# A polynomial over a polynomial after linear attention: one projected term, additions moved to accumulating DMAs, paired attention tiles, and a fixed issue order

## The chip, the cores and the metric

The kernel runs on one core of a Trainium2 chip. The metric is the device time of one execution in microseconds (us), lower being better. The core has a matrix engine (TensorE, PE in the profile for matmuls and PEld for weight loads), a vector engine (VectorE, DVE), a scalar engine (ScalarE, ACT), GpSimd (POOL), which issues the accumulating DMAs here, SyncE (SP), which issues the loads and stores, and 16 DMA engines that all queues share. Each engine works through its own list of instructions in order. Tiles lie in SBUF, the on-chip memory; TensorE's results land in PSUM, from where another engine copies them out (an "evacuation"). "Granted clock" is the share of TensorE's full clock that the profile shows as granted. Executions are called fast or slow: a run more than 1.5% above the fastest of the same kernel is slow.

## The reference, cut to what matters

```python
# attention: batch 4, heads 4, seq 1088, head_dim 32; S1, S2 are 8 x 32
phi(x) = outer(S1 @ x, S2 @ x)              # 64 features for each row
kv, z  = sum_s phi(k) v,  sum_s phi(k)
attn   = (phi(q) @ kv) / (phi(q) @ z + 1e-6)
# then, for x = attn as 4352 tokens x 128
h = x @ w_in                                # 128 -> 2048
P = a[0] + a[1]*h + a[2]*h**2 + a[3]*h**3
Q = 1 + |b[0]|*|h| + |b[1]|*h**2
out = (P / (Q + 1e-6)) @ w_out              # 2048 -> 128
```

All arrays come and go as float32. Between the two matmuls the kernels work in bfloat16.

## The kernel before

Tokens are taken in eight chunks of 512 and a last one of 256 (the last 64 rows of each batch). A "group" is eight blocks of 128 hidden columns of one chunk, as a tile of 128 x 4096. A few groups, the first and last ones, are smaller; all together are worth 17 full groups. For each group TensorE computes `h` (the "hidden products"), ScalarE copies it to bf16 (`hb`), VectorE makes the polynomials, and ScalarE makes the reciprocal as exp(-ln Q).

```python
# VectorE, for one group (names: m = |h|, u = Q - 1, y = numerator, r = 1/Q)
m = hb & 0x7FFF                                   # abs, by clearing the sign bit
u = m * b1 + b0                                   # tensor_scalar, two scalars
u = u * m                                         # tensor_tensor
y = hb * a3 + a2                                  # tensor_scalar
y = y * hb                                        # tensor_tensor
y = y + a1                                        # tensor_scalar
y = y * hb                                        # tensor_tensor
y = y * r                                         # tensor_tensor, after ScalarE's Ln and Exp
# TensorE: two terms are projected, a0 sits in the first weight
out_ps += (a0 * w_out).T @ r
out_ps += w_out.T @ y
...
# every copy from PSUM is ScalarE's; attention works on one-bank tiles (128 x 512), a pair of heads at a time
class Plan:                                       # a list scheduler at build time
    def issue(self):
        ...
        key = (t, s["rank"], s["n"])              # earliest start, then rank, then number
        ...
# hidden products of group g have rank g - 1.45, its last product g + 0.55
BUFS = dict(xT=3, hb=3, m=1, u=2, r=2, y=2, L=2, h_ps=2, out_ps=1, w_ps=2, kv_ps=1, ...)
```

## Time and profile before

| | before |
|---|---|
| time, median of the runs beside the changed kernel | 329.27 us (323.33 to 333.12, 4 runs; by the 1.5% rule three of them are slow) |
| span of the profiled execution | 323.9 us |
| VectorE busy | 286.5 us, 88% |
| TensorE busy (matmul records) | 280.0 us, 86% |
| ScalarE busy | 228.4 us, 71% |
| DMA engines, share of the steady part | 0.04 |

The page of the kernel before: the busy time of each engine, two rows of the 40 equal slices (a digit is the busy share in tenths), and the chain of waits followed back from the last instruction.

```profile
PE 280.0 (86%) x1153; PEld 150.0 (46%) x1172; DVE 286.5 (88%) x300; ACT 228.4 (71%) x213; POOL 8.7 (3%) x29
...
DVE  1461599999999999999999999999999999999990
...
DMA  5798000200020000000000000000000000000000
...
DVE 77%; PE 13%; DMA 5%; issue 1%; SPq 1%; ACT 1%; DVEq 0%
```

The reader is to see that VectorE is full from slice 6 to slice 39, that the DMA engines have next to nothing to do in that time, and that VectorE is 77% of the chain.

The groups by line of the kernel before, shapes kept apart: busy time, mean ns of one, then the idle time before them.

```profile
L503 DVE TENSOR_TENSOR y<-y,hb 128x4096 bf16<-128x4096 bf16 x30 | 68.7, 2292 | 0.9
L486 DVE TENSOR_TENSOR u<-u,m 128x4096 bf16<-128x4096 bf16 x15 | 34.4, 2292 | 0.4
L510 DVE TENSOR_TENSOR y<-y,r 128x4096 bf16<-128x4096 bf16 x15 | 34.3, 2284 | 0.0
L482 DVE TENSOR_SCALAR u<-m,b_abs 128x4096 bf16<-128x4096 bf16 x15 | 20.2, 1345 | 0.4
L499 DVE TENSOR_SCALAR y<-hb,a_sb 128x4096 bf16<-128x4096 bf16 x15 | 20.1, 1341 | 0.0
L506 DVE TENSOR_SCALAR y<-y,a_sb 128x4096 bf16<-128x4096 bf16 x15 | 19.3, 1286 | 0.5
L476 DVE TENSOR_SCALAR m<-hb 128x4096 int16<-128x4096 int16 x15 | 18.3, 1220 | 0.0
```

A pass with two tensors costs 2.29 us, one with scalars 1.22 to 1.35 us. Eight such passes are 14.35 us for a full group, with next to no idle time before them. This is what the change attacks.

The windows of the kernel before: each row gives its length and then each engine's busy time, the granted TensorE clock, the DMA share and GB/s, for the prologue, the steady part (from VectorE's first pass of group 0 to its last) and the end.

```profile
0.00:35.80 35.80, 30.81 (x144) 18.84 (x147) 11.39 (x34) 9.55 (x16) 6.62 (x27) 0.95 0.74 217
35.80:316.50 280.70, 247.54 (x1004) 130.46 (x1020) 275.12 (x267) 218.07 (x195) 2.09 (x2) 0.97 0.04 12
316.50:323.90 7.40, 1.70 (x6) 0.69 (x5) 0.00 (x0) 0.74 (x2) 0.00 (x0) 0.50 0.08 18
```

In the steady part VectorE (the third busy time of a row) works for 275.1 of 280.7 us.

### The profile page before, as it was taken

The numbers are of one execution on the slowest core, as the hardware profiler recorded it, in microseconds if no ns is written. First come the engines' busy times: TensorE is split into PE (matmuls) and PEld (weight loads), VectorE is DVE, ScalarE is ACT, GpSimd is POOL, SyncE is SP. The second block draws the span as 40 slices with busy tenths as digits, with TensorE's granted clock in tenths as the row PEclk, the third lists the DMA queues.
The fourth block names the chain that finished last, engine by engine and source line by source line (L and its number), as shares of the span: only waits on it lengthen the run. The fifth ranks groups of instructions, "written<-read, shape, count | busy, mean of one in ns | idle before, by whom it ended". The sixth has DMA issues, their size and how long they took to land.

```text
span 323.9 us, 3027 instructions
## 1 busy us (share of the span) xinstructions
PE 280.0 (86%) x1153; PEld 150.0 (46%) x1172; DVE 286.5 (88%) x300; ACT 228.4 (71%) x213; POOL 8.7 (3%) x29
## 2 busy tenths in 40 slices
PE   7969999988899999898999998979999975992532
PEld 4835455555443544555445554645345422650220
DVE  1461599999999999999999999999999999999990
ACT  3122678979479879794798888675989795686650
POOL 4102000002000000000000000000000000000000
PEclk9997999999999999999999999989999999698695
DMA  5798000200020000000000000000000000000000
GB/s 157 222 314 266 0 1 2 65 1 0 25 74 0 0 34 0 0 0 2 32 0 1 34 0 0 0 2 32 0 0 35 0 0 0 0 34 0 0 32 16
DMA packets 12125, 11.20 MB, mean 35 GB/s; under 512 B 4048, under 2 KB 10448, under 8 KB 11984
## 3 DMA queue, kind: packets, MB, share of 16 engines
q1 hardware_dynamic: 12112, 11.02, 11.2%
q8 instruction: 9, 0.15, 0.2%
q14 instruction: 4, 0.03, 0.0%
HBM read 8.79 MB, written 2.23 MB: 34 GB/s over the span
## 4 chain that ended last, share of the span: by engine, by line
DVE 77%; PE 13%; DMA 5%; issue 1%; SPq 1%; ACT 1%; DVEq 0%
DVE y L503 22%; DVE u L486 11%; DVE y L510 10%; DVE y L499 6%; DVE u L482 6%; DVE y L506 6%; PE h_ps L466 6%; DVE m L476 5%; DMA L<-in_moe_w_out_dram 3%; DVE q_pT L398 3%; DVE k_p L314 2%; PE out_ps L517 2%; PE w_ps L405 2%; DMA v_sb<-in_v_dram 2%; PE w_ps L389 2%; DVE x_sb L417 2%
## 5 line engine op out<-in xcount | busy, mean ns | idle before, releaser
L466 PE MATMUL h_ps<-xT,w_in_sb 128*128 128x512 f32 (+1 forms) x288 | 127.7, 584 | 2.7 <-ACT xT L428 2.4
L472 ACT CAST hb<-h_ps 128x1024 bf16<-128x1024 f32 x68 | 67.7, 1013 | 23.6 <-PE h_ps L466 22.8
L490 ACT ACTIVATE L<-u,one_ap 128x2048 f32<-128x2048 bf16 (+1 forms) x35 | 68.4, 1954 | 18.1 <-DVE u L486 18.1
L503 DVE TENSOR_TENSOR y<-y,hb 128x4096 bf16<-128x4096 bf16 (+2 forms) x40 | 78.9, 1972 | 1.2
L466 PEld LDWEIGHTS h_ps<-xT,w_in_sb 128*128 128x128 f32 x288 | 53.3, 194 | 56.3 <-issue 42.3
L495 ACT ACTIVATE r<-L 128x2048 bf16<-128x2048 f32 (+1 forms) x35 | 65.4, 1870 | 0.4
L517 PE MATMUL out_ps<-r,w_out_108 128*128 128x512 bf16 (+1 forms) x139 | 35.6, 378 | 11.6 <-ACT r L495 11.2
L517 PE MATMUL out_ps<-y,w_out_109 128*128 128x512 bf16 (+1 forms) x132 | 34.4, 389 | 10.7 <-DVE y L510 9.9
L486 DVE TENSOR_TENSOR u<-u,m 128x4096 bf16<-128x4096 bf16 (+2 forms) x20 | 39.4, 1971 | 0.6
L510 DVE TENSOR_TENSOR y<-y,r 128x4096 bf16<-128x4096 bf16 (+2 forms) x20 | 39.3, 1965 | 0.1
L517 PEld LDWEIGHTS <-w_out_109 128*128 128x128 bf16 x144 | 14.4, 104 | 32.1 <-issue 21.7
L517 PEld LDWEIGHTS <-w_out_108 128*128 128x128 bf16 x144 | 14.2, 102 | 32.1 <-issue 22.6
L476 DVE TENSOR_SCALAR m<-hb 128x4096 int16<-128x4096 int16 (+2 forms) x20 | 21.2, 1060 | 7.5 <-ACT hb L472 7.5
L482 DVE TENSOR_SCALAR u<-m,b_abs 128x4096 bf16<-128x4096 bf16 (+2 forms) x20 | 23.7, 1185 | 0.6
L499 DVE TENSOR_SCALAR y<-hb,a_sb 128x4096 bf16<-128x4096 bf16 (+2 forms) x20 | 23.6, 1181 | 0.0
L506 DVE TENSOR_SCALAR y<-y,a_sb 128x4096 bf16<-128x4096 bf16 (+2 forms) x20 | 22.5, 1126 | 0.7
L405 PE MATMUL w_ps<-kv_dup,q_pT 128*128 128x66 f32 x128 | 16.9, 288 | 5.4 <-DVE q_pT L398 5.4
L405 PEld LDWEIGHTS w_ps<-kv_dup,q_pT 128*128 128x128 f32 x128 | 16.6, 204 | 9.7 <-DVE q_pT L398 7.7
L328 PEld LDWEIGHTS kv_ps<-v_aug,k_p 128*128 128x128 f32 x128 | 16.3, 191 | 3.2 <-issue 1.9
L394 ACT COPY A_sb<-w_ps 128x512 f32<-128x512 f32 (+1 forms) x18 | 9.5, 564 | 10.7 <-PE w_ps L389 10.7
L389 PE MATMUL w_ps<-qT,Srep_106 64*128 64x512 f32 (+1 forms) x36 | 16.9, 615 | 0.1
L328 PE MATMUL kv_ps<-v_aug,k_p 128*128 128x66 f32 x128 | 16.2, 269 | 0.1
(70 smaller groups left out, 184.0 us busy)
## 6 DMA issues: line engine op xcount, KB each, us to landing
k_sb<-in_k_dram SPq DMA_DIRECT2D x4, 512.0 KB, 4.0
v_sb<-in_v_dram SPq DMA_DIRECT2D x4, 512.0 KB, 5.8
q_sb<-in_q_dram SPq DMA_DIRECT2D x4, 512.0 KB, 3.9
out_dram<-oT SPq DMA_DIRECT2D x8, 256.0 KB, 2.0
w_in_sb<-in_moe_w_in_dram SPq DMA_DIRECT2D x1, 1024.0 KB, 7.1
k_rem<-in_k_dram SPq DMA_DIRECT2D x4, 32.0 KB, 4.4
v_rem<-in_v_dram SPq DMA_DIRECT2D x4, 32.0 KB, 2.7
q_rem<-in_q_dram SPq DMA_DIRECT2D x4, 32.0 KB, 6.4
```

The costliest lines, as they stand in the source:

```text
L405: nc.tensor.matmul(nd_ps[r0:r1, i * 66:(i + 1) * 66], lhsT=T["q_pT", n, hp][:, i * 128 + r0:i * 128 + r1], rhs=kv_of(b, i, hp), start=True ...
L466: nc.tensor.matmul(T["h", g, s][:, i * W:(i + 1) * W], lhsT=w_in_sb[:, fi * 128:(fi + 1) * 128], rhs=T["xT", n][:, :W], start=True, stop=True)
L472: nc.scalar.copy(out=T["hb", g][:, s * W:(s + nsub) * W], in_=T["h", g, s])
L482: nc.vector.tensor_scalar(out=T["u", g][:, :gw], in0=T["m", g][:, :gw], scalar1=b_abs[:, 1:2], scalar2=b_abs[:, 0:1], op0=AX.mult, op1=AX.add)
L486: nc.vector.tensor_mul(out=T["u", g][:, :gw], in0=T["u", g][:, :gw], in1=T["m", g][:, :gw])
L490: nc.scalar.activation(out=T["L", g, l0][:, :lw], in_=T["u", g][:, l0:l0 + lw], func=ACT.Ln, bias=one_ap)
L495: nc.scalar.activation(out=T["r", g][:, l0:l0 + lw], in_=T["L", g, l0][:, :lw], func=ACT.Exp, scale=-1.0)
L499: nc.vector.tensor_scalar(out=T["y", g][:, :gw], in0=T["hb", g][:, :gw], scalar1=a_sb[:, 3:4], scalar2=a_sb[:, 2:3], op0=AX.mult, op1=AX.add)
L503: nc.vector.tensor_mul(out=T["y", g][:, :gw], in0=T["y", g][:, :gw], in1=T["hb", g][:, :gw])
L506: nc.vector.tensor_scalar(out=T["y", g][:, :gw], in0=T["y", g][:, :gw], scalar1=a_sb[:, 1:2], scalar2=None, op0=AX.add)
L510: nc.vector.tensor_mul(out=T["y", g][:, :gw], in0=T["y", g][:, :gw], in1=T["r", g][:, :gw])
L517: nc.tensor.matmul(T["o", n][:, :W], lhsT=W_terms[t][:, fis[i], :], rhs=src[:, i * W:(i + 1) * W], start=(t == 0 and fis[i] == 0), stop=(t ...
```

## The change

Its intent is to take work off VectorE without giving it to an engine that is nearly as full. The algebra: with x scaled by b1/b0, h' = h*b1/b0 gives Q - 1 = (b0*b0/b1) * (|h'| + h'*h'), so Ln takes the factor as its scale and the bracket needs only a square, an abs and an addition. The numerator is regrouped as (a3' h' + a2') * h'^2 + (a1' h' + a0), which reuses the square and includes a0, so that one term is projected. The two additions are done by DMAs that add their source to their destination in SBUF. Four further parts: attention works on two-bank PSUM tiles with both pairs of heads at once and masks the key sum once; 28 copies from PSUM go to VectorE; buffers are reshared; and the list scheduler gives way to a fixed list of 622 step numbers, said to come from annealing. Some of the matmuls on zeros that keep TensorE busy in the prologue also go (29 records before, 18 after).

```diff
-        def d_lin():   ... u = m * b1 + b0
-        def d_mul():   ... u = u * m
+        def d_sq():    nc.vector.tensor_mul(out=s, in0=hb, in1=hb)
         def d_abs():   (into u)
+        def add(dst, src, dma):
+            if dma:
+                nc.gpsimd.dma_start(out=d, in_=s, accum_op=AX.add, max_dma_last_dim=4096)
+            else:
+                nc.vector.tensor_add(out=d, in0=d, in1=s)          # add("u", "s"), add("t", "hb")
-        n_first, n_mul, n_add, n_mul, n_over
+        def d_high():  t  = hb * a3 + a2
+        def d_cube():  t  = t * s
+        def d_low():   hb = hb * a1 + a0
+        def d_over():  t  = t * u                                   # u now holds 1/Q
-        project(0, ...) with r and a0 * w_out;  project(1, ...) with y and w_out
+        project() with t and w_out
-    evac: nc.scalar.copy(...)
+    copy(name, out, in_)               # ScalarE, or VectorE where ENGINE names it
+U_DVE = []                             # groups whose additions stay on VectorE: none
+T_DVE = []
+ENGINE = {"k0.ev": "DVE", ..., "g0.e2": "DVE", "g2.e4": "DVE", ..., "o8.eT": "DVE"}    # 28 names
+ORDER = [31, 8, 7, 32, 34, 33, ..., 619, 620, 621]                                    # 622 numbers
-    plan.issue()
+    plan.issue(ORDER)
-BUFS = dict(xT=3, hb=3, m=1, u=2, r=2, y=2, L=2, h_ps=2, out_ps=1, w_ps=2, kv_ps=1, ...)
+BUFS = dict(xT=3, hb=3, s=2, u=3, t=3, L=2, h_ps=3, out_ps=1, w_ps=1, kT=1, a_t=1, k_p=1, A_sb=1, ...)
```

(The diff is cut to its core; the bodies of the passes are shortened to formulas.)

## The prediction

> **What bounds it now.** The page gives VectorE 88% busy (286.5 us of 323.9), PE 86%, ScalarE 71%. The chain of waits is 77% VectorE. The groups by line (shapes apart) show the eight vector passes of a full group of 128x4096: four tensor_tensor at 2.29 us, abs 1.22, two two-scalar passes at 1.34, one add at 1.29, together 14.3 us; over all groups 248.6 us. The other 38 us are attention. Before that stand 36 us of prologue (the first evacuated group reaches VectorE at 35.8 us), behind it 7.4 us of last projection, transposes and store.
>
> **What changes.** a0 goes into the numerator, so one product is projected: half of the projections go (about 144 x 0.23 = 30 us of PE). x is scaled so that the denominator is |h|+h^2. Per group VectorE keeps square, cube and final product (3 x 2.29), abs 1.22, two two-scalar passes (2 x 1.34): 10.8 us instead of 14.3, about 186 us in all. That saves 62 us. The two additions become accumulating DMAs, about 34 in full-group (1 MB) equivalents. Attention on VectorE: about 36 instead of 38 us. 28 copies go from ScalarE to VectorE: nine of 128x1024, ten of 128x512, some small; priced like the fp32 PSUM passes here (0.68 us for 512, about 1.2 for 1024), about 22 us. My sums: VectorE 245, ScalarE 208, PE about 240 (warm-up between matmuls removed too).
>
> **The DMAs.** The Trainium skill, "DMA: Bandwidth & Descriptors", section "Anatomy of one DMA", fits 2.0 us plus bytes/436 GB/s. An accumulate reads two streams; my estimate is 4.8 us of engine time and 6.8 us latency for 1 MB, so 165 to 200 us in all: busy 70 to 85% of the steady part, where DMA is now at 0 to 10% (slice rows). No trace here shows an accumulate. The same skill, "SBUF — State Buffer", section "Who interferes with whom", says that GpSimd cannot write descriptors while VectorE holds the shared port; three 1.2 to 1.35 us passes per group do that, so I expect an issue delayed by 1 to 2 us, mostly hidden: the fixed order puts some 19 us of vector work between square and final product, against about 8 us for the add and 7.8 us for two Ln/Exp pairs.
>
> **Time.** Prologue about 32 us (VectorE does about 15 of its 245 in it), 230 us of VectorE work with 5% bubbles, since four resources now sit at 80 to 90% with fixed orders and few buffers: 242; end about 8 us. I expect 281 us, 267 to 299. All of VectorE's saving lies on the critical path; PE's and ScalarE's does not by itself, but keeps them from becoming the limit. Chances: faster 0.95, same 0.03, slower 0.02.
>
> **What would show it.** VectorE busy near 245 and about 85% of the span; PE 240 or less; ScalarE 205 to 212; DMA slices near 7 to 9 tenths from 45 us to the end; Ln's wait changing from VectorE to DMA. The chain should alternate between VectorE, PE and a little DMA; DMA under 15% of it.
>
> **What would make it wrong.** (1) Accumulates much slower than 7 us (descriptor starvation, queueing behind the loads): then Ln and the final product wait for DMA in each group and the time goes to 300 or over. (2) VectorE passes slowed by GpSimd on the shared port. (3) A busier PE gets a lower granted clock (0.95 now). (4) One late DMA stops PE through the fixed order, as a single w_ps and out_ps buffer are left. (5) Better than thought: a prologue under 28 us and no bubbles, about 265.

## The result, and the profile after

The changed kernel took 275.5 us (median of 4 runs, 273.6 to 276.6, all fast) against 329.27 us before. Three of the four runs before are slow; in the rounds of the later experiments the fast runs of the kernel before took 323.2 to 327.0 us, so fast against fast the step is from about 324 us. A ratio here is the mean time of one kernel's fast runs over that of the other's of the same rounds, so it is not quite the ratio of the medians that are quoted: for the changed kernel it is 0.850, with a 95% interval of 0.846 to 0.855. The output is correct.

The page of the changed kernel: busy times, the same two rows of slices, the DMA queue of the additions (packets, MB, share of 16 engines' span), and the chain.

```profile
PE 238.0 (87%) x1004; PEld 131.9 (48%) x1017; DVE 236.9 (86%) x221; ACT 212.0 (77%) x168; POOL 61.6 (22%) x76
...
DVE  1575799799999799994999999999999999997671
...
DMA  5897559969699548999498889899999999999960
...
q0 software_dynamic: 9600, 35.65, 72.7%
...
DVE 39%; DMA 20%; PE 16%; ACT 16%; issue 6%; SPq 1%; DVEq 0%; POOLq 0%
```

VectorE's busy time fell by 49.6 us and TensorE's by 42 us, while the DMA engines went from idle to nearly full. No engine now dominates the chain.

The groups by line of the changed kernel, the six remaining passes of a full group:

```profile
L523 DVE TENSOR_TENSOR s<-hb 128x4096 bf16<-128x4096 bf16 x15 | 34.4, 2292 | 1.7 <-ACT hb L172 1.4
L542 DVE TENSOR_TENSOR t<-t,s 128x4096 bf16<-128x4096 bf16 x15 | 34.3, 2287 | 0.2
L556 DVE TENSOR_TENSOR t<-t,u 128x4096 bf16<-128x4096 bf16 x15 | 34.3, 2285 | 6.9 <-ACT u L553 6.9
L538 DVE TENSOR_SCALAR t<-hb,a_sb 128x4096 bf16<-128x4096 bf16 x15 | 21.1, 1408 | 0.0
L545 DVE TENSOR_SCALAR hb<-hb,a_sb 128x4096 bf16<-128x4096 bf16 x15 | 20.3, 1351 | 0.3
L526 DVE TENSOR_SCALAR u<-hb 128x4096 int16<-128x4096 int16 x15 | 18.3, 1220 | 0.3 <-ACT hb L172 0.2
```

Three passes of 2.29 us instead of four, three with scalars instead of four: 10.8 us a group. The final product waits 6.9 us in all for ScalarE, which in turn waits 12.6 us for the `u` additions (in all, times, longest):

```profile
ACT L L549 <- DMA u<-s: 12.6, 11, 4.0
```

The windows of the changed kernel, cut at the same events as before:

```profile
0.00:32.10 32.10, 28.95 (x165) 19.14 (x168) 17.19 (x37) 5.35 (x7) 6.41 (x28) 1.00 0.76 227
32.10:266.30 234.20, 207.37 (x834) 112.10 (x844) 218.82 (x182) 206.68 (x161) 55.14 (x48) 0.96 0.90 168
266.30:274.10 7.80, 1.70 (x6) 0.68 (x5) 0.85 (x2) 0.00 (x0) 0.00 (x0) 0.50 0.07 17
```

Of the 49.8 us between the two spans, 3.7 come from the prologue and 46.5 from the steady part; the end gave back 0.4. In the steady part VectorE has 56 us less work, but its idle time grew from 5.6 to 15.4 us.

The issues of the large additions in the changed kernel: count, KB, median us from issue to landing.

```profile
u<-s POOLq DMA_DIRECT2D x15, 1024.0 KB, 9.4
t<-hb POOLq DMA_DIRECT2D x15, 1024.0 KB, 9.2
```

They take 9.3 us to land. Their engine time is 72.7% of 274.1 us over 34 additions' worth of 1024 KB (35.65 MB), which is 5.86 us for each.

And three windows of the changed kernel that show how evenly it is loaded, in the two halves of the steady part and in the tail:

```profile
32.10:170.00 137.90, 129.14 (x528) 70.31 (x533) 127.94 (x103) 117.25 (x95) 33.69 (x29) 0.99 0.84 157
170.00:246.00 76.00, 66.83 (x264) 35.53 (x267) 75.30 (x60) 71.80 (x56) 15.93 (x13) 0.98 1.01 187
246.00:274.10 28.10, 13.09 (x50) 6.95 (x50) 16.44 (x24) 17.63 (x12) 5.53 (x6) 0.65 0.67 131
```

From 170 to 246 us VectorE is 99% busy, ScalarE 94% and TensorE 88%, with the DMA share at 1.01 (the share is made of summed packet times, and here it passes 1). The means after 246 us hide two stages: until 262 us ScalarE is still 99% busy (15.83 of 16.0 us), and until 258 us the DMA share stays above 1 (1.04 and 1.06 in two windows of 6 us). Only after 262 us is nothing full.

### The profile page after: what moved, and what is told of

Its sections match the earlier page's. It is cut to its first block, busy times and chain, and to the rows that moved or that the text cites. A ratio compares the mean times of both kernels' runs of the same rounds, so it can differ in the third digit from the quotient of the medians.

```text
span 274.1 us, 2743 instructions
## 1 busy us (share of the span) xinstructions
PE 238.0 (87%) x1004; PEld 131.9 (48%) x1017; DVE 236.9 (86%) x221; ACT 212.0 (77%) x168; POOL 61.6 (22%) x76
## 3 DMA queue, kind: packets, MB, share of 16 engines
q0 software_dynamic: 9600, 35.65, 72.7%
## 4 chain that ended last, share of the span: by engine, by line
DVE 39%; DMA 20%; PE 16%; ACT 16%; issue 6%; SPq 1%; DVEq 0%; POOLq 0%
DMA u<-s 15%; DVE t L542 8%; ACT L L549 7%; DVE t L556 7%; DVE s L523 6%; DVE t L538 5%; ACT u L553 5%; PE h_ps L513 5%; DMA t<-hb 5%; DVE u L526 4%; DVE hb L545 3%; PE out_ps L562 2%; PE h_ps L443 2%; ACT hb L172 2%; PE w_ps L380 2%
## 5 line engine op out<-in xcount | busy, mean ns | idle before, releaser
L549 ACT ACTIVATE L<-u,one_ap,lsc 128x2048 f32<-128x2048 bf16 (+1 forms) x35 | 71.6, 2046 | 12.7 <-DMA u<-s 12.6
L553 ACT ACTIVATE u<-L 128x2048 bf16<-128x2048 f32 (+1 forms) x35 | 65.2, 1864 | 0.9
L556 DVE TENSOR_TENSOR t<-t,u 128x4096 bf16<-128x4096 bf16 (+2 forms) x20 | 39.2, 1965 | 9.8 <-ACT u L553 6.9
L533 POOL DMA_DIRECT2D u<-s x20 | 24.1, 1220 | 104.0 <-DVE u L526 35.1
L562 PE MATMUL out_ps<-t,w_out 128*128 128x512 bf16 (+1 forms) x133 | 35.3, 398 | 13.0 <-DVE t L556 12.3
L533 POOL DMA_DIRECT2D t<-hb x20 | 24.3, 1214 | 76.0 <-ACT hb L172 28.5
L523 DVE TENSOR_TENSOR s<-hb 128x4096 bf16<-128x4096 bf16 (+2 forms) x20 | 39.4, 1970 | 1.8 <-ACT hb L172 1.4
L542 DVE TENSOR_TENSOR t<-t,s 128x4096 bf16<-128x4096 bf16 (+2 forms) x20 | 39.3, 1966 | 0.3
L538 DVE TENSOR_SCALAR t<-hb,a_sb 128x4096 bf16<-128x4096 bf16 (+2 forms) x20 | 24.6, 1231 | 1.5 <-PE out_ps L562 1.5
L545 DVE TENSOR_SCALAR hb<-hb,a_sb 128x4096 bf16<-128x4096 bf16 (+2 forms) x20 | 23.8, 1190 | 0.4
L174 DVE CAST hb<-h_ps 128x1024 bf16<-128x1024 f32 x9 | 10.8, 1215 | 1.2 <-PE h_ps L513 1.2
```

What stands on the lines that cost most here:

```text
L523: nc.vector.tensor_mul(out=new("s", g)[:, :gw], in0=h, in1=h)
L533: nc.gpsimd.dma_start(out=d, in_=s, accum_op=AX.add, max_dma_last_dim=4096)
L538: nc.vector.tensor_scalar(out=new("t", g)[:, :gw], in0=T["hb", g][:, :gw], scalar1=a_sb[:, 3:4], scalar2=a_sb[:, 2:3], op0=AX.mult, op1=AX ...
L542: nc.vector.tensor_mul(out=T["t", g][:, :gw], in0=T["t", g][:, :gw], in1=T["s", g][:, :gw])
L549: nc.scalar.activation(out=new("L", g, l0)[:, :lw], in_=T["u", g][:, l0:l0 + lw], func=ACT.Ln, bias=one_ap, scale=lsc)
L553: nc.scalar.activation(out=T["u", g][:, l0:l0 + lw], in_=T["L", g, l0][:, :lw], func=ACT.Exp, scale=-1.0)
```

## The experiments

Two questions are left. Which part of the change brings the time, and what limits the new kernel? All experiments but two start from the changed kernel. Each ratio is to the kernel before in the same rounds; the changed kernel's own is 0.850. Runs with a wrong result keep the changed kernel's order, which was not made for them.

### 1. Additions on VectorE

```diff
-U_DVE = []
-T_DVE = []
+U_DVE = list(range(20))
+T_DVE = list(range(20))
```

> All 40 additions on VectorE instead of as accumulating DMAs; the issue order, engines of the copies and everything else unchanged. VectorE gains two tensor_tensor passes per group, priced by the trace at 39.3 us each over all groups, so its busy time goes from 237 to about 315 us. Theory A (the accumulating DMAs are what makes the one-term form pay; VectorE is the limit): 335 to 350 us, slower than the kernel before. Rival B (the fixed order, the attention and the halved projection bring the gain, the place of the additions matters little): 300 us or less. DMA share falls to about 10 to 15%.

Measured: 349.05 us, ratio 1.071 (1.063 to 1.078). The page:

```profile
PE 263.5 (76%) x1004; PEld 142.2 (41%) x1017; DVE 314.2 (91%) x261; ACT 213.5 (62%) x168; POOL 14.3 (4%) x36
...
DVE 70%; PE 20%; ACT 4%; issue 3%; DMA 1%; SPq 0%; DVEq 0%
```

Theory A holds. Without DMAs the new form has eight passes, as many as the old one, but five instead of four of them have two tensors: 15.4 us a group in this run against 14.35. It pays only because two passes leave VectorE. With the additions on VectorE it is slower than the kernel before, in spite of half the projections and the new attention. The order was made for the other assignment and the granted clock fell to 0.885, but VectorE's 314 us of work alone exceed the changed kernel's whole time, so no order could save this form. This also answers a fear of the prediction: without any accumulating DMA the 128x4096 scalar passes take 1.39 us (t) and 1.34 us (hb), with them 1.41 and 1.35, so the DMAs hardly slow VectorE: no pass is more than 2% longer with them.

### 2. The new rational in the old kernel

The attention, list scheduler and ScalarE copies of the kernel before, with the new passes, DMAs and single projection:

```diff
 (kernel before)
-  abs, lin, mul / first, mul, add, mul, over / two projections
+  sq, abs, DMA add u / high, cube, low, DMA add t / over / one projection     # ranks and lead 1.45 as before
```

> The kernel before with only the rational function changed (one term, scaled x, accumulating DMAs, one projection); its attention, its list scheduler and its copies on ScalarE kept. VectorE busy should fall by about 60 us to about 226, PE by about 35 to about 245, ScalarE stays near 230. Theory A (the rational with DMA adds is the whole gain): 275 to 292 us. Rival D (without the fixed order and the rebalanced copies the new pipeline stalls): over 297 us.

Measured: 337.41 us, ratio 1.036 (1.026 to 1.045). VectorE was busy for only 223.8 us, 67% of the span. The waits:

```profile
DVE s L490 <- ACT hb L482: 43.8, 10, 9.5
DVE t L519 <- ACT u L516: 27.8, 7, 11.5
ACT hb L482 <- PE h_ps L476: 36.7, 26, 3.1
ACT L L513 <- DMA u<-s: 18.7, 8, 4.5
```

(A row says who waited for whom: us in total, times, longest.) VectorE has 63 us less to do and the kernel is slower. Part of it is seen at 196 us: ScalarE's list comes to an Ln whose `u` has not landed and waits 2.5 us, an evacuation of the next group stands behind it in that list, and VectorE starves. But ScalarE waited twice as long, 36.7 us, for hidden products of TensorE, so this is not the whole cause, and the run does not separate the two. One flaw of this run: the planner reserved GpSimd until an addition had landed, which distorted the planned order.

### 3. The same with a planner that knows the DMA queue

```diff
-  addition = one GpSimd step with a lag
+  addition = GpSimd step, then a step on a serial queue; buffers freed when it lands
-    FR = 1.45                       # lead of the hidden products, in groups
+    FR = 2.4                        # attention moved ahead by the same amount
```

> As moe_only (attention, scheduler and copies of the kernel before, new rational), but the planner now knows that the additions share one DMA queue and when a buffer that a DMA reads comes free, and hidden products and evacuations are ranked one group earlier (lead 2.4 groups instead of 1.45). Theory A (the new rational is the whole gain, moe_only lost it by a lead too short for the DMA round trip): 280 to 300 us. Rival D (one of the other parts, above all the hand-fixed order, is needed): 310 us or more. Busy times as in moe_only: VectorE 224, ScalarE 233, PE 245 to 276.

Measured: 309.32 us, ratio 0.947 (0.939 to 0.955), between the two expectations. Lead and queue model together are worth 28 us with the same work: the added latency of the additions has to be planned for. The result lies 0.7 us under rival D's range, and so nearer to it than to theory A. It is still 34 us from the changed kernel. VectorE 73%, TensorE 84%, ScalarE 75% busy: gaps, not work. I did not separate lead from queue model, nor search for a better lead. What remains between this run and the changed kernel is the attention, the buffers, the copies and the order; runs 4 and 5 take back the last two, and no run takes back the paired attention or the buffers alone.

### 4. The new kernel's work in a greedy order

```diff
-    plan.issue(ORDER)
+    plan.issue(plan.greedy(rank_of))     # earliest start, then rank; lead 2.4; queue model as in 3
```

The single buffers of the new kernel made such a rule run into a dead end when planning, so two orderings were added (remainder keys after the main keys of a batch, keys of a batch after the sums of the one before).

> All instructions, tile counts and engines of the changed kernel; only the issue order comes from a greedy list rule like that of the kernel before (earliest start first, then a rank by group), with the same lead of 2.4 groups and the same queue model. Theory A (work per engine decides): 276 to 290 us. Rival D (the annealed order is worth much with four resources near saturation and single buffers): 300 us or more. Busy times must stay at VectorE 237, ScalarE 212, PE 238 within 3%, apart from PE, whose times stretch when its clock falls.

Measured: 328.67 us, ratio 1.011 (1.005 to 1.018). The page and two windows, before and after the first evacuation into `hb` that VectorE makes (at 54.2 us; in the changed kernel at 30.8 us):

```profile
PE 254.6 (78%) x1005; PEld 141.5 (43%) x1017; DVE 238.5 (73%) x221; ACT 213.8 (65%) x168; POOL 58.8 (18%) x76
```

```profile
0.00:54.20 54.20, 41.05 (x177) 27.02 (x178) 18.36 (x37) 5.72 (x8) 9.08 (x33) 0.78 0.57 163
54.20:326.50 272.30, 213.53 (x829) 114.52 (x840) 220.18 (x184) 208.07 (x160) 49.67 (x43) 0.91 0.76 140
```

VectorE and ScalarE do the same work within 1%, and the whole gain is gone: 23.4 us of it in the prologue, 29 us after it (272.3 against 243.3 us from that event to the end). TensorE's records are 7% longer at a mean granted clock of 0.885 instead of 0.952. Part of the loss is this order's own: the added ordering holds the remainder keys' transposes until the main keys' product ends at 19.0 us, with TensorE idle for 4.8 us, and then their product stands on VectorE behind a weight cast that waits for its load until 21.2 us. Rival D holds in this sense: a poor order costs as much as the whole change brings. It does not say what the best simple rule would reach, and it does not credit annealing as such; a hand-made list might do as well.

### 5. The copies back on ScalarE

```diff
-ENGINE = {"k0.ev": "DVE", ...}      # 28 names
+ENGINE = {}
```

> The 28 copies moved to VectorE go back to ScalarE, order unchanged. VectorE busy 237 to about 215, ScalarE 212 to about 230. If VectorE alone bound the time, it would fall to about 262 us. My theory (VectorE, ScalarE, PE and DMA all close to their limit from 170 to 246 us) says 277 to 290 us, ScalarE becoming the limit.

Measured: 299.98 us, ratio 0.923 (0.918 to 0.928): a miss, 10 us above my range. VectorE's work fell to 216.4 us and ScalarE's rose to 229.9 us, as expected, but VectorE then waited 35.5 us for `hb` from ScalarE, and TensorE's clock fell to 0.908. The 18 us that ScalarE gained became 24 us of time. The list was made for the other assignment, so part of this may be the list and not the balance; the run can't tell them apart.

### 6. Half the columns of each addition

```diff
-                nc.gpsimd.dma_start(out=d, in_=s, accum_op=AX.add, ...)
+                nc.gpsimd.dma_start(out=T[dst, g][:, :gw // 2], in_=T[src, g][:, :gw // 2], accum_op=AX.add, ...)
```

> Each accumulating DMA handles only the first half of its columns (wrong result on purpose); the DMA engine time of the additions halves from about 199 to about 100 us, number of issues and everything else unchanged. Theory A (VectorE with ScalarE is the limit, the DMAs are hidden): 270 to 275 us. Rival C (the DMA engines, 97 to 103% busy from 170 to 246 us, are the limit or cause most of VectorE's 15 us of steady idle time and the slow tail): 255 to 264 us.

Measured: 264.74 us, ratio 0.815 (0.808 to 0.822), a wrong result. The median lies a hair above rival C's range and 5 us below theory A's. The windows:

```profile
32.10:170.00 137.90, 136.21 (x586) 76.94 (x593) 136.42 (x110) 127.89 (x101) 31.35 (x31) 1.00 0.47 95
170.00:246.00 76.00, 61.76 (x226) 31.29 (x228) 73.96 (x63) 72.14 (x56) 12.67 (x14) 0.97 0.51 105
```

Halving the additions thus gains about 11 us. From 32 to 170 us both VectorE and TensorE are now 99% busy, where they were 93 and 94%. The waits for `u` additions are gone from ScalarE's list.

### 7. Plain copies in place of additions

```diff
-                nc.gpsimd.dma_start(out=d, in_=s, accum_op=AX.add, max_dma_last_dim=4096)
+                nc.gpsimd.dma_start(out=d, in_=s, max_dma_last_dim=4096)
```

> The accumulating DMAs become plain copies of the same bytes over the same buffers (wrong result on purpose): number of issues, sizes and order unchanged. My prediction took an accumulate for two reads at 436 GB/s, 4.8 us of engine time per MB; measured are 5.86 (72.7% of 274.1 us over 34 MB). If a copy costs half of that or the 2.4 us of the rate alone, DMA share of the software queue falls to 30 to 40% and the time to about that of half_dma, 262 to 268 us. If copy and accumulate cost the same, share and time stay (72%, 275 us).

Measured: 266.21 us, ratio 0.815 (0.812 to 0.818), a wrong result. Two of its four timed runs count as slow (268.0 us), the profiled one too; only its DMA costs are read from that profile:

```profile
q0 software_dynamic: 9344, 35.65, 35.1%
...
u<-s POOLq DMA_DIRECT2D x15, 1024.0 KB, 5.0
t<-hb POOLq DMA_DIRECT2D x15, 1024.0 KB, 4.7
```

A copy costs 0.351 x 265.9 / 34 = 2.74 us of engine time, an addition of the same bytes 5.86 us, 2.1 times as much. The same number of bytes and issues at half the engine time gives the time of run 6. So it is the DMA engines' time on the additions that costs the 11 us, not the number of issues or of bytes. In both runs the landing time fell too, from 9.3 to below 5 us, so occupied engines and late landings are not told apart. The copies' issues were also shorter, a median of 0.70 us instead of 1.19, but those of run 6, at 0.86 us, give the same time.

### 8. One VectorE pass less

```diff
         def d_low():
-            nc.vector.tensor_scalar(out=hb, in0=hb, scalar1=a1, scalar2=a0, op0=AX.mult, op1=AX.add)
+            pass
```

> The pass a1*h+a0 is left out on VectorE (wrong result on purpose): 23.8 us less VectorE busy time, the same DMAs, ScalarE and PE work. If VectorE is the only limit: 252 to 257 us. If the DMA engines are the limit in the second half (0.99 to 1.03 busy from 170 to 246 us): 264 to 272 us, with DMA still at 1.0 there and more waits for DMA.

Measured: 272.01 us, ratio 0.837 (0.832 to 0.843), a wrong result. The time is at the upper edge of the second range. VectorE's busy time fell by 20.7 us (236.9 to 216.2) and the time by 3.5 us. The DMA share from 170 to 246 us was 1.03, as expected, but the waits for `u` did not grow (9.5 us instead of 12.6); the final product waited for ScalarE instead, 13.1 us instead of 6.9. In the kernel before, 77% of the chain was VectorE; here a microsecond of VectorE is worth about a sixth of one. The chain says who is left:

```profile
ACT 34%; DMA 25%; PE 20%; DVE 14%; issue 5%; SPq 1%; POOLq 0%; DVEq 0%; ACTq 0%
```

### 9. Both taken away

> Both takings-away at once (wrong result on purpose): 23.8 us less VectorE work and half the columns of each accumulating DMA. Alone they gave 272.0 and 264.7 us against 275.5. If VectorE and the DMA engines are the two limits, and each hid the other: 245 to 256 us. If PE (99% busy from 32 to 130 us in half_dma) or ScalarE (95% from 130 to 246 us) is right behind them: 257 to 264 us.

Measured: 261.43 us, ratio 0.809 (0.806 to 0.812), wrong (edits of runs 6 and 8 together).

```profile
32.10:170.00 137.90, 137.89 (x600) 78.01 (x599) 126.87 (x103) 128.75 (x103) 28.80 (x32) 1.00 0.49 97
```

TensorE is busy for 137.89 of 137.90 us and is 83% of this run's chain: with VectorE and the DMA engines relieved, it is TensorE that fills up. Taking 100 us of DMA time and 21 us of VectorE time away buys 14 us in all. My reading is that VectorE, the DMA engines and TensorE lie within about 5% of each other as limits, since 5% of time is all that was won before TensorE was full; ScalarE, 93% busy there and 96% from 170 to 246 us, is close behind.

### 10 to 12. Three attempts at a better kernel

Each leaves the result correct and moves a few additions back to VectorE.

```diff
 tail_dve:  U_DVE = T_DVE = [17, 18, 19]     # the three small groups at the end
 u6:        U_DVE = [6]                      # the addition that landed 12.3 us after its issue
 u468:      U_DVE = [4, 6, 8]
```

> Only the additions of the last three small groups go to VectorE (a 2048, two 1024 columns: 3.8 us... of added VectorE work: 2 x (1.22 + 0.69 + 0.69) = 5.2 us). From 246 us on VectorE is idle for a quarter of the time and the chain shows waits for these DMAs. If DMA latency sets the end: 268 to 273 us. If the end is set by VectorE or ScalarE work: 275 to 280 us.

Measured: 278.81 us, ratio 0.857 (0.850 to 0.864). Not better: VectorE was 93% busy (20.4 of 22.0 us) from 246 to 268 us, its last final product ended at 267.4 instead of 266.3 us, and the span was 1.5 us longer. ScalarE's work in that stretch was the same as before (17.6 us).

> A correct variant: only the u addition of group 6 goes to VectorE. In the changed kernel this DMA, issued at 106.0 us, landed at 118.3 us, and ScalarE waited 4.0 us and VectorE later 2.7 us for it; VectorE pays 2.29 us. If that one late DMA costs what its waits say: 271 to 274.5 us. If the DMA queue as a whole sets the pace: no change, 275 to 277 us.

Measured: 276.12 us, ratio 0.853 (0.851 to 0.855): the same as the changed kernel. ScalarE's waits for the `u` DMAs fell from 12.6 to 7.5 us, but it now waited 4.8 us for VectorE's own addition, 12.3 us in all. VectorE's waits for ScalarE fell from 6.9 to 4.8 us, and VectorE paid a 2.29 us pass for it.

> A correct variant: the u additions of groups 4, 6 and 8 go to VectorE (each landed 9.4 to 12.3 us after its issue with ScalarE waiting). VectorE pays 6.9 us, the DMA queue is freed of 17.6 us. If the DMA queue is the tighter of the two limits: 269 to 274 us. If VectorE is: 277 to 283 us.

Measured: 279.14 us, ratio 0.863 (0.859 to 0.867): slower by about 1.5%. The gain of relieving the queue and the price on VectorE do not cancel; VectorE is the dearer of the two. Note the asymmetry: 6.9 us of passes put on VectorE cost about 4 us, 20.7 us taken off bought 3.5 (run 8), both in the same list. No run that keeps the result correct beats the changed kernel.

## Why the prediction was right, point by point

The time was forecast as 281 us, 267 to 299, and measured as 275.5 us.

- **The limit before.** "The chain of waits is 77% VectorE", eight passes at 14.3 us a group: the profile after has six at 10.8 us, as costed, at nearly unchanged durations (the one exception is a two-scalar pass of 1.41 us, costed at 1.34). The VectorE busy time fell by 49.6 us and the profiled span by 49.8 us. That the two agree so well is partly luck: VectorE's idle time grew by 9.8 us in the steady part and happened to shrink by 9.5 us in the prologue.
- **VectorE 245 us** was measured as 236.9 us. The term that was mis-sized is the attention, for which I forecast 2 us less. Counted by records (number times mean of each group of instructions), the six passes took 187.7 us (forecast 186), the copies 23.8 us (forecast 22), and attention with set-up fell from 49 to 37 us, by 12 us. My 38 us for the attention before was the page's 286.5 us less the passes' total; the page counts overlapping records once, and the overlap, 11.5 us before and 11.7 us after, had been taken off the attention.
- **Prologue 32, end 8 us**: 32.1 and 7.8 us. **Steady part 242 us with 5% bubbles**: 234.2 us with 6.6%. VectorE's work in it was 218.8 us instead of 230, which is 11 us less, and idle time of 15.4 instead of 12 us took back 3 of them.
- **TensorE about 240, ScalarE 205 to 212**: 238.0 and 212.0 us. Danger (3), a lower granted clock for a busier TensorE, did not come: it was 86 and 87% busy at a clock of 0.954 and 0.952.
- **The DMAs** were the term taken most from a page. The Trainium skill, "DMA: Bandwidth & Descriptors", section "Anatomy of one DMA", fits 2.0 us plus bytes at 436 GB/s. For a plain 1024 KB copy this gives 4.4 us, and run 7 shows 4.7 to 5.0 us. My step "an accumulate reads two streams", 4.8 us of engine time and 6.8 us latency, was too low: 5.86 us and 9.3 us. That the cost is about two copies (2 x 2.74 us = 5.5 us) agrees with the trace; the rest of the latency was not taken apart. Danger (1) thus came true in size, at 9.3 us, and not in its consequence: the given order left room, and ScalarE waited 12.6 us in all. The DMA part of the chain was 20%, not under 15%.
- **Descriptor starvation.** The same skill, "SBUF — State Buffer", section "Who interferes with whom", has GpSimd blocked while VectorE holds the shared port. In the trace an issue takes a median of 1.19 us and at most 2.17 us: 27 of the 30 large ones took 1.19 to 1.47 us, three 1.95 to 2.17 us. So an issue was mostly not lengthened, and at most by about 1 us, where 1 to 2 us was forecast; no run shows that the port is the cause of the three.
- **"All of VectorE's saving lies on the critical path"** was right for the step made, as far as run 1 shows it (77 us of added passes, 74 us of added time, at a lower granted clock), but not for one more step (run 8).
- **What the prediction left out** is the order. It counted on "5% bubbles" because the list was given. Runs 3 and 4 show that this was the most fragile number in it: with the same work, bubbles of 19% of the steady part can be had as well (VectorE busy for 220 of 272 us in run 4).

## What to carry to other kernels

When one engine is the limit and the DMA engines are idle, an elementwise addition of two SBUF tiles can be given to an accumulating DMA; it costs two copies' worth of DMA time and, here, 9 us of latency, so it must be issued well ahead (run 3 planned with a lead of 2.4 groups instead of 1.45), and it is worth arranging every in-order list so that nothing useful stands behind its consumer. Moving work to other engines ends when all of them are equally full: measure that by taking work away from one at a time, and then from two, as the share of the chain alone does not tell what the next microsecond is worth. After a change of latency, plan the order anew before judging the change; the same instructions took 275 or 329 us.

## What the Trainium skill lacked or had wrong

- "DMA: Bandwidth & Descriptors": it says that accumulating DMAs must be issued from GpSimd, but has no rate for them. Here 1024 KB of bf16, SBUF to SBUF, costs 5.86 us of all 16 engines (5.9 in runs 2 to 5 as well) and lands after 9.3 us in a busy queue; a plain copy issued in the same way costs 2.74 us and lands after 4.7 to 5.0 us, near the page's fit of 4.4 us.
- "SBUF — State Buffer", the summary rules: the advice not to hide a GpSimd-issued DMA under VectorE work does not forbid this use. With VectorE 93% busy over the steady part, 40 such issues took a median of 1.19 us and at most 2.17 us, and VectorE's passes were at most 2% longer than without any (1.41 against 1.39 us).
- "TensorE: Matmul & The Clock Gate", section "Part 1: The HAM clock gate", says that the clock halves after an idle window of about 3.4 us. The tail agrees: after 3.1 us of idle time eight projections of 512 columns took 1.90 us, after 6.2 us of it the same eight took 3.57 us. A size that the page does not have is what the order of a kernel limited by several engines does to it: with the same instructions the mean granted clock was 0.952 with the fixed list and 0.885 with the greedy one.
